# Chunked attention and a feed-forward layer on one core: weights in become float16 in the second group, those out in the third, on ACT and DVE

## The chip, the core and the metric

The kernel runs on one core of a Trainium2 chip. The core has five engines with instruction queues of their own: PE (TensorE, matmuls), DVE (VectorE), ACT (ScalarE), POOL (GpSimd) and SP (SyncE, which here issues all DMAs). The metric is device time in microseconds (us) of one execution; lower is better. One profiled execution of each kernel gives the rows that are read here. In them "PEld" is the loading of a matmul's stationary operand, a name such as `wh` is a tile with its buffer number left out, `out<-in` says what an instruction writes and reads, and L449 is line 449 of the kernel that the row is of.

## The reference

Attention inside chunks of 64 positions, followed by a feed-forward layer without bias over all 4608 tokens (8 batches of 576, with 8 heads of 64, so 512 features; 2048 hidden features), all in float32:

```python
scores = (q_c @ k_c.T) / sqrt(64)                 # per head and chunk of 64
attn = exp(scores - max(scores)); attn = attn / (sum(attn) + 1e-9)
x = (attn @ v_c)                                  # as [4608, 512]
h = x @ w_in                                      # [512, 2048]
g = h - tanh(h)
out = g @ w_out                                   # [2048, 512]
```

## The kernel before

The tokens are 36 tiles of 128, each a pair of chunks, in nine groups of four tiles (`SIZES`). In a group the hidden features are walked in 16 chunks of 128 (`fc`). For every chunk `gemm1` makes `ph` (128 hidden features by 512 tokens), `shrink` makes `t = h - tanh(h)` (tanh on ACT, subtraction on DVE) and splits it into a high part `gh` (ACT) and a low part `gl` (DVE), and `gemm2`, two chunks later (`LAG`), adds the chunk's product with `w_out` into four accumulators `po`, one for each tile. At the group's end `finish` copies the four accumulators out of PSUM (two on ACT, two on DVE) into tiles named `t` and stores them.

Single precision comes from two parts and three products: high by high, high by low, low by high. So a block of `gemm1` is 12 matmuls (3 products by 4 slices of the 512 features, L449) and a block of `gemm2` is 12 (3 products by 4 tiles, L478); both are 128x128 by 512. In groups 0 and 1 the parts are float32 tiles read as fp32r (`wt[fc][0]` and `[1]`, tiles `wh` and `wl`, each with both weights: part 0 of `w_in`, part 1 of `w_out`). From group 2 on all parts are float16, scaled by powers of two: the weights stand in `half_w[fc]`.

`Half.convert(fc)` makes those float16 weights, and all of them are made during group 1. For each of the two weights POOL adds the high and the low fp32r part back to one float32 (L405; into the attention's `s` buffers for the first three chunks, later into the `wl` tile of the chunk before, which is free by then), ACT rounds the scaled sum to the float16 high part (L409), and DVE takes the difference for the low part (L410), both into the `wh` tile. Two further freed `wl` tiles become second buffers of the attention's split `q` and `v`; POOL clears them (L259).

The attention of a group is computed during the group before it, in steps that stand between the blocks (`interleaved`): `sums` takes the spread of the next `q`, `k` (ACT, L99, whose elementwise result is thrown away into a tile named `a`) and `v` (DVE, L116), POOL takes the maximum over partitions (L106) and DVE makes scales of it (L110 to L112, L279); `split` makes float16 parts of `q` (L289, L290), `k` (L292, L293) and `v` (L298, L299); `scores` (L307, 24 matmuls); `softmax` (L313 to L321); `transpose` splits the weights into `a` (L327, L328) and has a DMA transpose it into an `s` tile (L330); `values` (L341, 24 matmuls) and L344, L345 write `x` for the next group. `k16` and `a` have one buffer each, `s` has two, `t` three.

The order of the first part is written out (`PLAN`); for the rest, and for ACT and DVE throughout, a scheduler places instructions by its own reckoning, and each engine then runs its list in order. PE's list before reads, at the start of each group, three blocks of L449 in a row, and from then on blocks of L478 and L449 by turns, with the attention's pieces between them. Before group 1 the weights are unpacked from 64-bit words (`weights`, L132 to L138): L137 (ACT) makes the high part and L138 (DVE) the low one, for one weight or for both at a time.

Of the kernel before, what the change touches and what calls it, by code (L numbers as in the profile page):

```python
# [22 lines left out]
P = 128  # L23
H = 8
# [32 lines left out]
def attn_ffn_kernel(ctx: ExitStack, tc: tile.TileContext, qE, kE, vE, qL, kL, vL, w_in, w_out, out):  # L57
# [19 lines left out]
    wt, half_w, w_pool = [[None, None] for _ in range(FC)], [None] * FC, {}  # L77

    def weight_tiles(pool, fcs):
        for fc in fcs:  # L80
            w_pool[fc] = pool
            for i, a in enumerate("hl"):
                wt[fc][i] = pool.tile([P, 2, DM], F32R, name=f"w{a}{fc}")
# [43 lines left out]
    def weights(pool, fc, parts):  # L127
# [8 lines left out]
        h, l = (t[:, parts] for t in wt[fc])  # L136
        nc.scalar.copy(out=h, in_=w.bitcast(F32))  # L137
        nc.vector.tensor_sub(l, w.bitcast(F32), h)  # L138
# [103 lines left out]
    class Late:  # L242
# [4 lines left out]
        def __init__(self, pool):  # L247
# [3 lines left out]
            self.v16, self.q16 = [], []  # L251
# [13 lines left out]
        def sums(self, g, n):  # L265
# [16 lines left out]
        def split(self, g, p, i):  # L282
# [8 lines left out]
            kk = d["k"] = self.pool.tile([P, 2, H, CH], F16, name="k16", bufs=1)  # L291
# [31 lines left out]
        def transpose(self, p):  # L323
# [5 lines left out]
            aT = self.pool.tile([P, H, CH], F32, name="s", bufs=2).bitcast(F16).rearrange("p h k -> p (h k)").rearrange("p (i q) -> p i q", i=8)  # L329
# [36 lines left out]
    class Half:  # L366
# [29 lines left out]
        def convert(self, fc):  # L396

            h, l = wt[fc]
            if fc < 3:
                w = [self.pool.tile([P, H, CH], F32, name="s", bufs=2).rearrange("p h k -> p (h k)") for _ in range(2)]  # L400
            else:
                t = w_pool[fc - 1].tile([P, 2, DM], F32R, name=f"wl{fc - 1}").bitcast(F32)
                w = [t[:, part] for part in range(2)]
            for part in range(2):
                nc.gpsimd.tensor_add(w[part], h[:, part].bitcast(F32), l[:, part].bitcast(F32))  # L405
            half = half_w[fc] = w_pool[fc].tile([P, 2, DM], F32R, name=f"wh{fc}").bitcast(F16).rearrange("p part (a n) -> p part a n", a=2)
            for part in range(2):
                to = self.to[:, part:part + 1]
                nc.scalar.activation(half[:, part, 0], w[part], AF.Copy, scale=to)  # L409
                nc.vector.scalar_tensor_tensor(out=half[:, part, 1], in0=w[part], scalar=to, in1=half[:, part, 0], op0=ALU.mult, op1=ALU.subtract)  # L410
# [16 lines left out]
    class FeedForward:  # L427
# [25 lines left out]
        def shrink(self):  # L453
            fc, t0, t1, n, ph = self.ph
            t = ffn.tile([P, MOST], F32, name="t", bufs=3)[:, :n]
            if self.half:
# [5 lines left out]
            if self.half:  # L462
# [50 lines left out]
    x, nx = new_x(), new_x()  # L513
    ff = FeedForward(0, x)
# [134 lines left out]
```

## Time and profile before

| | before |
| --- | --- |
| time, median of 3 runs | 886.29 us (885.56 to 889.21) |
| the profiled execution's own time | 889.29 us |
| its span, first to last instruction | 887.3 us |
| mean granted clock of PE | 0.989 |
| PE busy | 853.9 us (96%), 5163 matmuls |
| DVE busy | 597.3 us (67%) |
| ACT busy | 482.5 us (54%) |
| POOL busy | 60.4 us (7%) |
| DMA | 62.72 MB, mean 71 GB/s |

Busy times are shares of a program with unlike stages. Matmuls are pipelined, so a busy PE is not yet PE at its best pace; what a stage loses is seen in what PE waits for and in the granted clock, stage by stage. The columns of a group row ("engine op names shapes xcount | busy, mean ns | idle before, releaser") give in the last place how long the engine stood idle just before such instructions and what ended the idle time.

### The profile page before, as it was taken

Reading aid. Unit: us, or ns where it says so; the run is one execution under the profiler, and the core shown is the slowest. Engines: PE = TensorE matmul, PEld = TensorE weight load, DVE = VectorE, ACT = ScalarE, POOL = GpSimd, SP = SyncE. Lnnn points to the kernel's source line nnn. Section 1 sums busy time; section 2 is a strip of 40 time slices with the busy share of each in tenths; the row PEclk is TensorE's granted clock in tenths of the full one; section 3 lists DMA queues with packets and bytes.
Section 4 is the critical chain, followed back from the end, with each engine's and each line's share of the span. In section 5 each row is a group of like instructions: output and inputs, shape, how many; then the busy total and the mean of one; then the engine's idle time right before and its main releaser. Section 6 shows DMA issues by size and latency. Waiting matters only on the chain.

```text
span 887.3 us, 13178 instructions
## 1 busy us (share of the span) xinstructions
PE 853.9 (96%) x5163; PEld 487.2 (55%) x5165; DVE 597.3 (67%) x980; ACT 482.5 (54%) x840; POOL 60.4 (7%) x55
## 2 busy tenths in 40 slices
PE   9999999989689999999999999999999999999997
PEld 6888787867544544454445544454445444544443
DVE  6988795899978766667666766676666666543322
ACT  7798775654476537454645474447444744433222
POOL 0000011655310000000000000000000000000000
PEclk8999999999989999999999999999999999999999
DMA  9983434122123213111311132112221011001001
GB/s 236 256 211 110 160 120 142 48 50 59 24 74 82 60 36 107 37 49 36 106 48 49 36 84 70 49 37 60 84 60 37 13 49 24 13 13 48 1 1 48
DMA packets 61374, 62.72 MB, mean 71 GB/s; under 512 B 32640, under 2 KB 40832, under 8 KB 61312
## 3 DMA queue, kind: packets, MB, share of 16 engines
q1 hardware_dynamic: 61312, 61.88, 24.5%
q8 instruction: 40, 0.66, 0.3%
q14 instruction: 22, 0.18, 0.1%
HBM read 45.09 MB, written 9.44 MB: 61 GB/s over the span
## 4 chain that ended last, share of the span: by engine, by line
PE 68%; DVE 17%; DMA 5%; ACT 4%; issue 4%; SPq 1%; POOL 0%; ACTq 0%; POOLq 0%; DVEq 0%
PE ph L449 32%; PE po L478 30%; DVE wh L410 2%; DMA s<-a 2%; DMA out<-t 2%; PE psa L307 2%; PE psa L341 1%; PE psa L232 1%; ACT a L99 1%; DVE q16l L290 1%; DVE gl L470 1%; DVE v16l L299 1%; PE psa L184 1%; DVE t L461 1%; DMA k<-kE 1%
## 5 line engine op out<-in xcount | busy, mean ns | idle before, releaser
L449 PE MATMUL ph<-xh,wh 128*128 128x512 f16 (+2 forms) x1488 | 344.1, 379 | 9.3 <-DVE t L461 5.9
L478 PE MATMUL po<-wh,gh 128*128 128x512 f16 (+1 forms) x1024 | 319.2, 383 | 12.6 <-ACT gh L469 8.8
L478 PE MATMUL po<-wh,gl 128*128 128x512 f16 (+1 forms) x576 | 221.2, 385 | 2.9 <-DVE gl L465 2.9
L449 PEld LDWEIGHTS <-wh 128*128 128x128 f16 x1344 | 130.3, 98 | 157.9 <-issue 4.7
L457 ACT ACTIVATE t<-ph,sig 128x512 f32<-128x512 f32 x112 | 76.5, 683 | 139.1 <-PE ph L449 119.9
L458 DVE SCALAR_TENSOR_TENSOR t<-ph,sig,t 128x512 f32<-128x512 f32 x112 | 83.4, 745 | 96.6 <-ACT t L457 96.3
L478 PEld LDWEIGHTS <-gh 128*128 128x128 f16 x896 | 85.2, 98 | 103.1 <-ACT gh L464 6.3
L465 DVE SCALAR_TENSOR_TENSOR gl<-t,to_g,gh 128x512 f16<-128x512 f32 x112 | 84.1, 751 | 82.0 <-ACT gh L464 80.4
L464 ACT ACTIVATE gh<-t,to_g 128x512 f16<-128x512 f32 x112 | 80.7, 721 | 98.2 <-PE po L478 85.4
L478 PEld LDWEIGHTS <-gl 128*128 128x128 f16 x448 | 43.8, 98 | 57.6 <-DVE gl L465 5.4
L478 PE MATMUL po<-wl,gh 128*128 128x512 f32 x128 | 51.4, 402 | 0.0
L327 ACT CAST a<-s 128x512 f16<-128x512 f32 x28 | 17.3, 618 | 52.6 <-DVE s L321 52.6
L405 POOL TENSOR_TENSOR wl<-wh,wl 128x512 f32<-128x512 f32 x26 | 40.3, 1568 | 38.1 <-PE po L478 31.0
L449 PE MATMUL ph<-xh,wl 128*128 128x512 f32 (+1 forms) x144 | 36.3, 374 | 0.1
L449 PE MATMUL ph<-xl,wh 128*128 128x512 f32 (+1 forms) x144 | 36.2, 374 | 0.0
L469 ACT CAST gh<-t 128x512 fp32r<-128x512 f32 (+1 forms) x36 | 20.5, 570 | 24.6 <-DVE t L461 18.5
L106 POOL PARTITION_ALL_REDUCE xtop<-sums x7 | 2.6, 375 | 452.2 <-ACT a L99 446.1
L478 PEld LDWEIGHTS po<-wh,gh 128*128 128x128 f32 x128 | 24.6, 192 | 15.2 <-ACT gh L469 10.6
L449 PEld LDWEIGHTS ph<-xh,wh 128*128 128x128 f32 x144 | 24.8, 188 | 13.2 <-DVE t L461 7.2
L470 DVE TENSOR_TENSOR gl<-t,gh 128x512 fp32r<-128x512 f32 (+1 forms) x36 | 25.7, 713 | 7.1 <-ACT gh L469 6.8
L315 ACT ACTIVATE s<-s,exp 128x512 f32<-128x512 f32 x28 | 20.0, 713 | 18.5 <-DVE s L314 18.4
L449 PEld LDWEIGHTS ph<-xl,wh 128*128 128x128 f32 x144 | 26.0, 192 | 5.0
(120 smaller groups left out, 1068.1 us busy)
## 6 DMA issues: line engine op xcount, KB each, us to landing
out<-t SPq DMA_DIRECT2D x36, 256.0 KB, 2.2
raw<-w_in SPq DMA_DIRECT2D x16, 512.0 KB, 4.4
raw<-w_out SPq DMA_DIRECT2D x16, 512.0 KB, 6.8
rawk<-kL SPq DMA_DIRECT2D x28, 256.0 KB, 2.7
rawv<-vL SPq DMA_DIRECT2D x28, 256.0 KB, 2.6
xl<-qL SPq DMA_DIRECT2D x28, 256.0 KB, 2.7
qbd<-qE SPq DMA_DIRECT2D x16, 128.0 KB, 6.3
k<-kE SPq DMA_DIRECT2D x8, 256.0 KB, 6.0
```

The lines of the kernel that those rows point to most:

```text
L307: nc.tensor.matmul(ps[:, h], lhsT=q[a][:, h], rhs=d["k"][:, b, h], start=(k == 0), stop=(k == 2))
L315: nc.scalar.activation(s, s, AF.Exp, scale=d["exp"])
L405: nc.gpsimd.tensor_add(w[part], h[:, part].bitcast(F32), l[:, part].bitcast(F32))
L410: nc.vector.scalar_tensor_tensor(out=half[:, part, 1], in0=w[part], scalar=to, in1=half[:, part, 0], op0=ALU.mult, op1=ALU.subtract)
L449: nc.tensor.matmul(ph, lhsT=self.weight(fc, 0, a)[:, kc * P:(kc + 1) * P], rhs=x[b][:, kc, cols], start=(k == 0), stop=(k == 3 * KC - 1))
L457: nc.scalar.activation(t, ph, AF.Tanh, scale=self.sig)
L458: nc.vector.scalar_tensor_tensor(out=t, in0=ph, scalar=self.sig, in1=t, op0=ALU.mult, op1=ALU.subtract)
L464: nc.scalar.activation(gh, t, AF.Copy, scale=self.to_g)
L465: nc.vector.scalar_tensor_tensor(out=gl, in0=t, scalar=self.to_g, in1=gh, op0=ALU.mult, op1=ALU.subtract)
L469: nc.scalar.copy(out=gh, in_=t)
L470: nc.vector.tensor_sub(gl, t, gh)
L478: nc.tensor.matmul(self.po[t], lhsT=gg[a][:, ts], rhs=self.weight(fc, 1, b), start=(fc == 0 and i == 0), stop=(fc == FC - 1 and i == 2))
```

## The change

Weights are kept as one tile for each weight and part of a chunk (`wt[fc][part]` is a pair of tiles of 512 columns), where one tile held both weights. `weights` therefore makes high and low part of `w_in` and of `w_out` by instructions of their own.

`w_in` alone is converted in group 1, `w_out` in group 2. So group 2 runs its first product on float16 and its second on fp32r (`self.half` is a pair of flags). `convert` no longer has POOL add the parts: ACT makes the float16 high part from the scaled fp32r high part, DVE takes the difference, and a second DVE instruction adds the scaled fp32r low part to it. The result goes into the tile of the chunk before that held the low part (`place_of`), so the tiles of the high parts come free instead. Of the fourteen `w_in` tiles that are freed so, six become the attention's second buffers (`v16`, `q16`, and two for `k16`), two the places for its transposed weights (`aT`), four the places of the outputs (`outs`), one the place for L99's unused result (`junk`), and one the first place for `w_out`.

```diff
+            for part in range(2):
+                wt[fc][part] = [pool.tile([P, DM], F32R, name=f"w{a}{part}{fc}") for a in "hl"]
+    def place_of(a, part, fc, dtype=F16):
+        return w_pool[fc].tile([P, DM], F32R, name=f"w{a}{part}{fc}").bitcast(dtype)
...
-        h, l = (t[:, parts] for t in wt[fc])
-        nc.scalar.copy(out=h, in_=w.bitcast(F32))
-        nc.vector.tensor_sub(l, w.bitcast(F32), h)
+        for part in range(2)[parts]:
+            h, l = wt[fc][part]
+            w = ws[fc][:, part].bitcast(F32)
+            nc.scalar.copy(out=h, in_=w)
+            nc.vector.tensor_sub(l, w, h)
...
-                junk = self.pool.tile([P, 2, H * CH], F16, name="a", bufs=1).bitcast(U8).rearrange("p a (b n) -> p (a b) n", b=2)
+                junk = self.pool.tile([P, 2, H * CH], F16, name="a", bufs=1).bitcast(U8).rearrange("p a (b n) -> p (a b) n", b=2) if self.junk is None else self.junk
...
-            aT = self.pool.tile([P, H, CH], F32, name="s", bufs=2).bitcast(F16).rearrange("p h k -> p (h k)").rearrange("p (i q) -> p i q", i=8)
+            aT = self.aT[p % 2] if self.aT else self.pool.tile([P, H, CH], F32, name="s", bufs=2).bitcast(F16).rearrange("p h k -> p (h k)").rearrange("p (i q) -> p i q", i=8)
...
-                nc.gpsimd.tensor_add(w[part], h[:, part].bitcast(F32), l[:, part].bitcast(F32))
-            half = half_w[fc] = w_pool[fc].tile([P, 2, DM], F32R, name=f"wh{fc}").bitcast(F16).rearrange("p part (a n) -> p part a n", a=2)
-            for part in range(2):
-                to = self.to[:, part:part + 1]
-                nc.scalar.activation(half[:, part, 0], w[part], AF.Copy, scale=to)
-                nc.vector.scalar_tensor_tensor(out=half[:, part, 1], in0=w[part], scalar=to, in1=half[:, part, 0], op0=ALU.mult, op1=ALU.subtract)
+        def convert(self, part, fc, place):
+            half_w[part][fc] = place.rearrange("p (a n) -> p a n", a=2)
+            (h, l), (h16, l16), to = wt[fc][part], (half_w[part][fc][:, i] for i in range(2)), self.to[:, part:part + 1]
+            h, l = h.bitcast(F32), l.bitcast(F32)
+            nc.scalar.activation(h16, h, AF.Copy, scale=to)
+            nc.vector.scalar_tensor_tensor(out=l16, in0=h, scalar=to, in1=h16, op0=ALU.mult, op1=ALU.subtract)
+            nc.vector.scalar_tensor_tensor(out=l16, in0=l, scalar=to, in1=l16, op0=ALU.mult, op1=ALU.add)
...
+            self.half = g > 1, g > 2
...
-                ot = ffn.tile([P, DM], F32, name="t", bufs=3)
+                ot = outs[t] if outs else ffn.tile([P, DM], F32, name="t", bufs=3)
...
-                at[2 * fc + 2 * LAG + 1].append(lambda fc=fc: half.convert(fc))
-            at[2 * LAG + 4].append(lambda: att.room(half.spare(0), half.spare(1)))
+                at[2 * fc + 1].append(lambda fc=fc: half.convert(0, fc, place_of("l", 0, fc - 1) if fc else first_place))
...
+                t = [place_of("h", 0, fc) for fc in (range(6) if k == 0 else range(6, 13))]
+                if k == 0:
+                    att.room(t[0:2], t[2:4])
+                    att.k16 += [a.rearrange("p (a h c) -> p a h c", a=2, h=H) for a in t[4:6]]
+                else:
+                    att.aT += [a.rearrange("p (i q) -> p i q", i=8) for a in t[0:2]]
+                    outs.extend(a.bitcast(F32) for a in t[2:6])
+                    att.junk = t[6].bitcast(U8).rearrange("p (a n) -> p a n", a=MOST // P)
+            at[12].append(lambda: more(0))
+            at[2 * FC + 2].append(lambda: more(1))
+        if g == 2:
+            for fc in range(FC):
+                at[2 * fc + 2 * LAG + 1].append(lambda fc=fc: half.convert(1, fc, place_of("l", 1, fc - 1) if fc else place_of("h", 0, 13)))
```

Instructions move, because the scheduler decides anew. PE's list is the same from the start of group 1 on, block by block. Three other places follow; line numbers of the changed kernel are its own (L457 and L466 are the old L461 and L470, L408 and L409 the two new DVE conversions, L103 the old L99, L453 and L460 the old L457 and L464, L500 the old L504).

DVE in group 1, the first softmax of the attention there, before:

```order
L461 TENSOR_TENSOR t<-ph,t 128x512
L314 TENSOR_TENSOR s<-psa,mx 128x512
L293 SCALAR_TENSOR_TENSOR k_1802<-rawk,to,k_1802 128x512
L470 TENSOR_TENSOR gl<-t,gh 128x512
L317 TENSOR_REDUCE sm<-s 128x8
L410 SCALAR_TENSOR_TENSOR wh_1812<-wl_1809,to_w,wh_1812 128x512
L318 TENSOR_SCALAR sm<-sm 128x8
```

and now, to where the attention's `a` is made:

```order
L409 SCALAR_TENSOR_TENSOR wl_1851<-wl_95,to_w,wl_1851 128x512
L324 TENSOR_SCALAR sm<-sm 128x8
L296 SCALAR_TENSOR_TENSOR q16l<-xl,to,q16h 64x8x64
L466 TENSOR_TENSOR gl<-t,gh 128x512
L325 RECIPROCAL sm<-sm 128x8
L408 SCALAR_TENSOR_TENSOR wl_1890<-wh_98,to_w,wl_1890 128x512
L326 TENSOR_SCALAR sm<-sm 128x8
L299 SCALAR_TENSOR_TENSOR wh_1818<-rawk,to,wh_1818 128x512
L327 TENSOR_TENSOR s<-s,sm 128x512
L457 TENSOR_TENSOR t<-ph,t 128x512
L409 SCALAR_TENSOR_TENSOR wl_1890<-wl_99,to_w,wl_1890 128x512
L334 TENSOR_TENSOR a<-s,a 128x512
```

The conversions read the weights' own tiles instead of a sum from POOL, there are two for a chunk of one weight, and `a` (L334) stands behind the next chunk's subtraction and a conversion.

POOL in group 1, before:

```order
L405 TENSOR_TENSOR s<-wh_70,wl_71 128x512 x2
L106 ISA
L106 ISA xtop<-sums 128x3
L405 ISA
L405 TENSOR_TENSOR s<-wh_72,wl_73 128x512 x2
L259 MEMSET wl_1655 128x1024 x2
L259 MEMSET wl_1656 128x1024 x2
L405 TENSOR_TENSOR s<-wh_74,wl_75 128x512 x2
```

and now:

```order
L265 MEMSET wh_1814 128x1024
L265 MEMSET wh_1815 128x1024
L110 ISA xtop<-sums 128x3
L265 MEMSET wh_1816 128x1024
L265 MEMSET wh_1817 128x1024
```

The additions are gone, 32 in all; the maximum of the spreads (`xtop`) stands between MEMSETs.

ACT at the end of a group (3, with float16 on both products), before, from the spreads to the last `gh` (three rows of the attention and the copies of the outputs, L504, stand behind it):

```order
L99 ACTIVATE a,sums<-xl 128x2048
L99 ACTIVATE a,sums<-rawk 128x2048
L457 ACTIVATE t<-ph,sig 128x512
L289 ACTIVATE q16h<-xl,to 64x8x64 x2
L464 ACTIVATE gh<-t,to_g 128x512
L292 ACTIVATE k_4326<-rawk,to 128x512
L298 ACTIVATE v16h<-rawv,to 64x8x64
L457 ACTIVATE t<-ph,sig 128x512
L298 ACTIVATE v16h<-rawv,to 64x8x64
L289 ACTIVATE wl_1656<-xl,to 64x8x64 x2
L464 ACTIVATE gh<-t,to_g 128x512
```

and now the last two chunks:

```order
L453 ACTIVATE t<-ph,sig 128x512
L460 ACTIVATE gh<-t,to_g 128x512
L453 ACTIVATE t<-ph,sig 128x512
L460 ACTIVATE gh<-t,to_g 128x512
L304 ACTIVATE wh_1814<-rawv,to 64x8x64
L350 ACTIVATE xh<-psa 128x4x128
L304 ACTIVATE wh_1814<-rawv,to 64x8x64
L500 ACTIVATE wh_2453<-po_3418,undo_g 128x512
```

The spreads now stand in mid-group, at the eighth chunk or so, and the splits of the next group's pairs follow them there; the last two chunks have `t` and `gh` next to each other, and the outputs (`wh_2453`) have tiles of their own.

More of the change, by code (lines that the diff above doesn't have):

```diff
@@ L73, in attn_ffn_kernel @@
     ps_a = ctx.enter_context(tc.tile_pool(name="ps_a", bufs=2, space=PSUM))
-    wt, half_w, w_pool = [[None, None] for _ in range(FC)], [None] * FC, {}
+    wt, half_w, w_pool = [[None, None] for _ in range(FC)], [[None] * FC for _ in range(2)], {}
     def weight_tiles(pool, fcs):
@@ L427, in attn_ffn_kernel, with __init__ @@
     class FeedForward:
-        def __init__(self, g, x, half=None):
-            self.g, self.x, self.queue, self.po, self.half = g, x, [], [], half
-            if half:
+        def __init__(self, g, x):
+            self.g, self.x, self.queue, self.po = g, x, [], []
+            self.half = g > 1, g > 2
+            if g > 1:
                 self.sig, self.to_g, self.undo_g = half.power_of(g)
         def weight(self, fc, part, i):
-            return half_w[fc][:, part, i] if self.half else wt[fc][i][:, part]
+            return half_w[part][fc][:, i] if self.half[part] else wt[fc][part][i]
         def room(self, pool, tiles):
@@ L455, in shrink @@
             t = ffn.tile([P, MOST], F32, name="t", bufs=3)[:, :n]
-            if self.half:
+            if self.half[0]:
                 nc.scalar.activation(t, ph, AF.Tanh, scale=self.sig)
@@ L461, in shrink @@
                 nc.vector.tensor_sub(t, ph, t)
-            if self.half:
+            if self.half[1]:
                 gh, gl = (ffn.tile([P, MOST], F32R, name=f"g{a}").bitcast(F16)[:, :n] for a in "hl")
@@ L498, in finish @@
             for t in range(SIZES[self.g]):
-                ot = ffn.tile([P, DM], F32, name="t", bufs=3)
-                if self.half:
+                ot = outs[t] if outs else ffn.tile([P, DM], F32, name="t", bufs=3)
+                if self.half[1]:
                     if t % 2:
@@ L513, in attn_ffn_kernel @@
     x, nx = new_x(), new_x()
+    outs = []
     ff = FeedForward(0, x)
@@ L587, in attn_ffn_kernel @@
         for part in range(2):
-            nc.scalar.activation(junk, wt[fc][0][:, part].bitcast(F32), AF.Square, accum_out=sums_w[part][:, fc:fc + 1])
+            nc.scalar.activation(junk, wt[fc][part][0].bitcast(F32), AF.Square, accum_out=sums_w[part][:, fc:fc + 1])
     ff.finish()
@@ L595, in attn_ffn_kernel @@
         x, nx = nx, new_half_x() if g + 1 < NG else None
-        ff = FeedForward(g, x, half if g > 1 else None)
+        ff = FeedForward(g, x)
         ff.room(ps_o1, range(2))
```

19 lines of the change are left out of this document (4 added, 15 removed).

## The prediction

> **What bounds the kernel now.** I first cut the span into groups of four token tiles, since one busy share mixes stages with different limits. The cuts are the places where the trace has three L449 blocks in a row, which is how a group begins. Columns of the table by stretches: length, busy time with instruction count of PE, PEld, DVE, ACT and POOL, granted clock, DMA share, GB/s.
>
> ```profile
> core 0: us, PE busy (x) PEld busy (x) DVE busy (x) ACT busy (x) POOL busy (x), PEclk, DMA share, GB/s
> 141.25:256.64 115.39, 101.13 (x577) 79.30 (x575) 100.43 (x140) 66.23 (x105) 50.93 (x36) 0.96 0.20 52
> 160.68:239.90 79.22, 72.17 (x446) 56.94 (x444) 77.80 (x96) 44.44 (x72) 45.24 (x31) 0.98 0.21 50
> 256.64:347.82 91.18, 89.44 (x577) 43.17 (x577) 68.19 (x118) 54.74 (x81) 2.87 (x3) 1.00 0.25 70
> 347.82:438.95 91.13, 88.98 (x577) 43.02 (x576) 58.92 (x103) 47.71 (x71) 0.37 (x1) 1.00 0.20 59
> 438.95:529.61 90.66, 88.99 (x578) 43.01 (x576) 58.93 (x103) 47.72 (x71) 0.37 (x1) 1.00 0.21 59
> ...
> 710.93:799.41 88.48, 88.48 (x577) 43.16 (x576) 50.76 (x86) 38.14 (x58) 0.00 (x0) 1.00 0.10 25
> ```
>
> The rows are group 1, a piece of it, and groups 2, 3, 4 and 7 (5 and 6 repeat 4's 90.66). All have the same 577 matmuls. Group 7 runs PE without a pause: 88.48 us is the floor of a float16 group. Groups 2 to 6 are 2.2 to 2.7 us above it, group 1 is 26.9 us above. In group 1's inner 79 us DVE is busy 98% of the time: there DVE is the bound, elsewhere PE is.
>
> Next, what PE waits for, in group 1 (first three rows) and after it (last three): microseconds in total, times, longest.
>
> ```profile
> PE po L478 <- ACT gh L469: 7.2, 2, 4.2
> PE ph L449 <- DVE t L461: 5.9, 2, 3.1
> PE psa L341 <- DMA s<-a: 1.0, 1, 1.0
> ...
> PE po L478 <- ACT gh L464: 3.8, 5, 0.8
> PE po L478 <- DVE gl L465: 2.9, 5, 0.6
> PE ph L449 <- DVE t L458: 2.2, 5, 0.8
> ```
>
> Group 1 loses 14.1 us in five waits. It loses more than the waits: three stretches right behind the longest of them run at half clock (last of the columns but two), and PE's rows show one such idle time.
>
> ```profile
> 244.04 0.80 PE L478 MATMUL po<-wh,gh 128*128 128x512 f32 x1 [4.17 <-ACT gh L469]
> ...
> 185.85:189.26 3.41, 3.41 (x17) 2.42 (x16) 3.41 (x6) 1.14 (x3) 0.42 (x1) 0.50 0.26 77
> 243.88:247.29 3.41, 3.25 (x8) 2.47 (x9) 2.24 (x4) 1.34 (x3) 0.00 (x0) 0.50 0.40 77
> 254.12:257.53 3.41, 3.41 (x10) 1.97 (x9) 2.85 (x6) 2.07 (x5) 0.00 (x0) 0.50 0.27 104
> ```
>
> Three times 3.41 us at half speed cost 5.1 us. 115.39 - 14.1 - 5.1 = 96.2 us is what group 1 needs without them.
>
> **Why DVE is full.** The same DVE operations cost differently in group 1 (first two rows) and in group 4 (last two).
>
> ```profile
> L410 DVE SCALAR_TENSOR_TENSOR wh<-wl,to_w,wh 128x512 f16<-128x512 f32 x24 | 23.5, 1008 | 0.1
> L293 DVE SCALAR_TENSOR_TENSOR k<-rawk,to,k 128x512 f16<-128x512 f32 x4 | 4.0, 1010 | 0.0
> ...
> L465 DVE SCALAR_TENSOR_TENSOR gl<-t,to_g,gh 128x512 f16<-128x512 f32 x16 | 12.0, 751 | 9.5 <-ACT gh L464 9.2
> L293 DVE SCALAR_TENSOR_TENSOR k<-rawk,to,k 128x512 f16<-128x512 f32 x4 | 3.0, 739 | 0.0
> ```
>
> L293 is the same instruction at 739 and at 1010 ns. What differs is POOL, which adds halves of weights in group 1 (50.93 us busy) and rests later. The order of time shows that it is POOL's additions and not its clearing of buffers:
>
> ```profile
> 163.33 3.11 POOL L405 TENSOR_TENSOR s<-wh,wl 128x512 f32<-128x512 f32 x2 [7.05 <-DVE t L461]
> 166.38 3.62 POOL L259 MEMSET wl<- 128x1024 f16 x4
> ...
> 163.50 3.48 DVE L299 SCALAR_TENSOR_TENSOR v16l<-rawv,to,v16h 64x512 f16<-64x512 f32 x2
> 168.22 1.41 DVE L410 SCALAR_TENSOR_TENSOR wh<-s,to_w,wh 128x512 f16<-128x512 f32 x2
> ```
>
> Two operations beside two additions take 3.48 us; two beside the MEMSETs 1.41. The page "SBUF — State Buffer" of the Trainium skill (section "Who interferes with whom") says the same: a DVE operation with two SBUF inputs blocks only against a GpSimd operation that reads SBUF. The trace agrees (1.74 us each against 0.71).
>
> How much it is: group 4's DVE time, 58.93, plus 30 conversions at 0.751 (22.5) is 81.4 us. Measured are 100.43, so some 19 us in group 1 are lengthening.
>
> **The change, part by part.**
>
> (1) *Group 1.* All 32 POOL additions go. DVE keeps 32 conversion instructions there (two for each of 16 chunks instead of one for each of 32), so its work is 58.9 + 32 x 0.751 = 82.9 us against 96.2 us of PE: 86% where it was saturated. The new order spreads them two or three to a chunk, and a chunk's `gl` is wanted only four blocks of 12 matmuls (11 us) after its `ph`. POOL keeps four MEMSETs, which the row above clears of blame. I take all five waits and all half clocks as gone, but leave 0.8 us, for L341's wait hangs on a transposing DMA as much as on DVE: 97.0 us, which is -18.4. Bounds: 94.9 (32 blocks at 2.79 and eight attention pieces at 0.70, rows below; -20.5) and half of the loss staying (-9).
>
> (2) *Group 2.* The second product now runs on the unconverted fp32r weights. Chain of waits, a block of 12 in fp32r, one in float16, and an attention piece:
>
> ```profile
> 152.64 2.79 PE ph L449 x12
> ...
> 268.22 2.59 PE ph L449 x12
> 270.81 0.70 PE psa L307 x24
> ```
>
> 16 blocks x 0.20 = +3.2 us on PE, nothing hides that. The page "TensorE: Matmul & The Clock Gate" of the Trainium skill (section "Back-to-back issue gap") gives N/2.4 + 2.5 ns between matmuls without regard to the type, 216 ns for both; by it this term would be zero and the forecast 858 us. Here the rows say 216 (2.59/12) and 233 (2.79/12), and the rows decide.
>
> The 32 new DVE instructions (24.0 us) and 16 ACT ones go on top of group 4's load: 82.9 of DVE in some 92 us, 90%. PE covers them so long as DVE is not lengthened; with POOL idle it is not. If that cover failed, each microsecond of DVE over 92 would show. So group 2 is 88.48 + 3.2 + 0.5 for its edges = 92.2, or +1.0. Bounds: +0.3 and +13 (rival 2).
>
> (3) *Group edges.* The end of group 2 and the start of 3, on SP, ACT, DVE and PE:
>
> ```profile
> 329.09 1.23 SPq L330 DMA_TRANSPOSE s<-a  x1
> 332.22 1.91 ACT L99 ACTIVATE a<-xl 128x2048 uint8<-128x2048 f32 x1 [1.57 <-DMA s<-a]
> 336.81 0.17 DVE L110 TENSOR_SCALAR from<-xtop 128x3 f32<-128x3 f32 x1 [5.38 <-POOL xtop L106]
> 344.47 0.60 PE L478 MATMUL po<-wh,gh 128*128 128x512 f16 x2 [0.72 <-ACT gh L464]
> 345.65 0.39 PE L478 MATMUL po<-wh,gl 128*128 128x512 f16 x1 [0.58 <-DVE gl L465]
> 352.45 0.69 ACT L457 ACTIVATE t<-ph,sig 128x512 f32<-128x512 f32 x1 [4.39 <-DMA out<-t]
> 353.98 2.32 PE L449 MATMUL ph<-xh,wh 128*128 128x512 f16 x10 [0.81 <-DVE t L458]
> ```
>
> Two chains end here. L99 writes its unused result over `a` and so waits for the transposing DMA; behind it POOL's maximum and DVE's L110 are late (DVE stands 5.38 us), and the split of the next pair falls into the last two chunks, ahead of `gh`. And the outputs take the three `t` buffers, so the next group's first tanh waits 4.39 us for their DMAs. The change gives L99 a place of its own, and the ACT order shows it moved from two chunks before the end to mid-group, the splits with it; the outputs get four places. Late next: nothing up to group 7's floor. I take 89.0 us for groups 3 to 6, leaving 0.5 each: -2.1 for group 3, -1.7 for each of 4, 5 and 6. Bounds: 0 and 2.2 each.
>
> (4) *The end.* PE's last matmul and the last copy:
>
> ```profile
> 882.08 0.38 PE L478 MATMUL po<-wh,gl 128*128 128x512 f16 x1
> ...
> 883.46 0.75 DVE L502 TENSOR_SCALAR t<-po,undo_g 128x512 f32<-128x512 f32 x1 [1.50 <-DMA out<-t]
> ```
>
> PE is done at 882.46; the copy starts 1.0 later because its buffer waits for the first output's DMA. With four places: -1.0, nothing left to wait for but PE.
>
> (5) *The start.* Weight halves become separate tiles, so nine DVE subtractions of 1024 columns become 18 of 512:
>
> ```profile
> L138 DVE TENSOR_TENSOR wl<-w,wh 128x1024 fp32r<-128x1024 f32 x9 | 10.9, 1220 | 1.4 <-ACT wh L137 1.4
> L138 DVE TENSOR_TENSOR wl<-w,wh 128x512 fp32r<-128x512 f32 x14 | 9.5, 688 | 2.6 <-ACT wh L137 2.4
> ```
>
> 9 x (2 x 0.688 - 1.220) = 1.4 us more DVE work while it is nearly full, against an earlier start of the first product, which waits for one half only. Between -1 and +1.4 I take +0.5.
>
> Sum: 0.5 - 18.4 + 1.0 - 2.1 - 5.1 - 1.0 = -25.1. The profiled execution has a span of 887.3 and a time of 889.29, some 3 us over the median of 886.29; the difference is taken from the median: 861 us.
>
> **The rivals.**
>
> *Rival 1: only group 1 gains.* The edges stay, since the last `gh` and `gl` of a group are a chain of four dependent operations whatever stands before them. For it: PE's 0.72 + 0.58 there have no DMA in them. Against: group 7's edge has the same chain and no wait (88.48). Without the 7.2 us of part 3: 868 us.
>
> *Rival 2: DVE stays the bound.* The lengthening has another cause than POOL, perhaps the fp32r traffic, and follows the conversions into group 2. Then DVE needs 58.9 + 32 x 1.008 + 11.6 (what is left of the 19 us once the conversions' 30 x 0.257 are counted at their own) = 102.8 us in both groups, with two half-clock stretches (3.4) in each: group 1 106 (-9), group 2 106 (+15); with parts 3 to 5 (-7.7) 884 us, no change that can be told. Against it: the MEMSET row, and group 4's 739 ns.
>
> *Rival 3: slower, by late transposes.* In the new order the attention's `a` in groups 1 and 2 stands behind a conversion and the next chunk's subtraction, and its DMA takes 3 us more. If PE then stands at L341 for over 3 us, as in the 4.17 row, it also loses half of 3.41: 4.8 us a pair. It turns the sign when six of the eight pairs do so (6 x 4.8 = 29 > 25.1); with all eight 899 us. For it: the one L341 wait above. Against: that was 1.0 us with DVE saturated.
>
> *Rival 4: the change does not free POOL or the edges in time*, because the scheduler puts conversions where a place is not yet free. Each such wait would be a row of DVE waiting for PE; I see no such row in the new order, and give it a price of half of part 1: 870 us.
>
> **How the numbers follow.** Forecast 0.64; rival 1 0.16, rival 2 0.06, rival 3 0.05, rival 4 0.09. The predicted time is the forecast's, 861. Its own bounds reach from 855 (the floor in groups 1 and 3 to 6) to 866. The range takes in rivals 1 and 4 and some better luck at the start: 853 to 874. This kernel's runs can tell 0.5%, 4.4 us, from no change. Faster by more: forecast, rivals 1 and 4, and some of rival 2, 0.90. Within: the rest of rival 2 and little else, 0.05. Slower: rival 3, 0.05.
>
> **What would show it.** Right: POOL without additions; L293 near 740 ns in group 1; PE's waits in group 1 under 2 us in all and no stretch at clock 0.50 in it; group 1 near 97, group 2 near 92, groups 3 to 6 near 89; DVE's wait for `xtop` under 2 us; no tanh waiting for an output's DMA. Wrong: DVE operations still at 1 us in groups 1 or 2 (rival 2), the edges still at 90.7 (rival 1), waits of L341 for the transposing DMA (rival 3), DVE waiting for PE before a conversion (rival 4), or a group 1 that starts more than 2 us later than 141.25.

## The result, and the profile after

Measured side by side, before took 887.0 us (median of 4 runs, 885.56 to 889.21) and the changed kernel **860.42 us** (median of 4, 857.21 to 861.19): ratio 0.969, 95% interval 0.966 to 0.973. The forecast was 861. The profiled execution of the changed kernel took 861.19 us, with a span of 859.4 against 887.3 before.

The same cut into groups, at the three L445 blocks in a row (L445 is the old L449, L474 the old L478). The rows are groups 1, 2, 3, 4 and 7 and the rest; 5 and 6 are 88.48 too.

```profile
core 0: us, PE busy (x) PEld busy (x) DVE busy (x) ACT busy (x) POOL busy (x), PEclk, DMA share, GB/s
142.72:237.82 95.10, 95.10 (x577) 76.87 (x576) 88.02 (x162) 65.65 (x102) 5.20 (x6) 1.00 0.27 77
237.82:329.97 92.15, 92.15 (x578) 59.27 (x577) 77.14 (x133) 55.58 (x86) 0.37 (x1) 1.00 0.21 58
329.97:418.46 88.49, 88.49 (x578) 43.18 (x578) 59.32 (x100) 47.82 (x71) 0.37 (x1) 1.00 0.22 63
418.46:506.94 88.48, 88.48 (x578) 43.19 (x577) 59.34 (x101) 48.07 (x71) 0.37 (x1) 1.00 0.21 60
...
683.90:772.38 88.48, 88.48 (x578) 43.17 (x577) 49.32 (x82) 37.63 (x57) 0.00 (x0) 1.00 0.10 25
772.38:859.40 87.02, 83.04 (x385) 37.45 (x383) 26.29 (x35) 24.16 (x35) 0.00 (x0) 1.00 0.06 24
```

In groups 1 to 7 the length and PE's busy time are now one number, at clock 1.00: PE runs from 142.72 to its last matmul without a pause (the last row goes on for 4 us behind that matmul). These groups have the same matmuls and differ by the type that they multiply: both products in fp32r (95.10), the second alone (92.15), none (88.48). PE's list of waits holds 4.8 us in all (the two longest of its rows are shown; the other four are 2.5 of that):

```profile
PE ph L541 <- DVE warm L519: 1.2, 1, 1.2
PE po L474 <- ACT gh L465: 1.1, 3, 0.5
...
DVE from L114 <- POOL xtop L110: 3.2, 6, 0.6
```

These waits lie ahead of group 1, since from there to the last matmul PE is busy without a break. The last row is DVE's: L114 (the old L110) waited 0.6 us at most for POOL's maximum, where one such wait was 5.38 us. And the chain of work that ended last, on the profile's page, is PE's for 93% of the span, where it was 68% before:

```profile
PE 93%; DVE 5%; ACT 1%; issue 1%; DMA 0%; SPq 0%; DVEq 0%
```

DVE in group 1, by line, with the instructions that used to be lengthened:

```profile
L409 DVE SCALAR_TENSOR_TENSOR wl<-wl,to_w,wl 128x512 f16<-128x512 f32 x15 | 11.2, 747 | 0.1
L408 DVE SCALAR_TENSOR_TENSOR wl<-wh,to_w,wl 128x512 f16<-128x512 f32 x15 | 11.1, 739 | 1.0 <-ACT wl L407 1.0
L466 DVE TENSOR_TENSOR gl<-t,gh 128x512 fp32r<-128x512 f32 x16 | 10.9, 683 | 0.5 <-ACT gh L465 0.5
L457 DVE TENSOR_TENSOR t<-ph,t 128x512 f32<-128x512 f32 x16 | 10.9, 681 | 0.5 <-ACT t L456 0.4
L120 DVE TENSOR_REDUCE sums<-rawv 128x1 f32<-128x2048 f32 x2 | 4.6, 2286 | 1.4 <-DMA rawv<-vL 1.4
L296 DVE SCALAR_TENSOR_TENSOR q16l<-xl,to,q16h 64x512 f16<-64x512 f32 x6 | 4.5, 746 | 0.1
L296 DVE SCALAR_TENSOR_TENSOR wh<-xl,to,wh 64x512 f16<-64x512 f32 x6 | 4.5, 745 | 0.1
...
L299 DVE SCALAR_TENSOR_TENSOR wh<-rawk,to,wh 128x512 f16<-128x512 f32 x5 | 3.7, 746 | 0.1
```

L299 is the L293 of before: 746 ns here, 1010 there. Where the time went, from the two tables by groups (profiled executions):

| | before | after | difference | forecast |
| --- | --- | --- | --- | --- |
| start of group 1 | 141.25 | 142.72 | +1.5 | +0.5 |
| group 1 | 115.39 | 95.10 | -20.3 | -18.4 |
| group 2 | 91.18 | 92.15 | +1.0 | +1.0 |
| group 3 | 91.13 | 88.49 | -2.6 | -2.1 |
| groups 4 to 6, together | 271.98 | 265.44 | -6.5 | -5.1 |
| group 7 | 88.48 | 88.48 | 0 | 0 |
| group 8 to the end of the span | 87.9 | 87.02 | -0.9 | -1.0 |
| span | 887.3 | 859.4 | -27.9 | -25.1 |

### The profile page after: what moved, and what is told of

It reads as the page before. It is cut to its first block, busy times and chain, and to the rows that moved or that the text cites. A ratio compares the mean times of both kernels' runs of the same rounds, so it can differ in the third digit from the quotient of the medians.

```text
span 859.4 us, 13143 instructions
## 1 busy us (share of the span) xinstructions
PE 850.5 (99%) x5163; PEld 503.1 (59%) x5165; DVE 593.9 (69%) x1021; ACT 483.5 (56%) x849; POOL 12.2 (1%) x23
## 4 chain that ended last, share of the span: by engine, by line
PE 93%; DVE 5%; ACT 1%; issue 1%; DMA 0%; SPq 0%; DVEq 0%
PE po L474 42%; PE ph L445 41%; PE psa L347 2%; PE psa L313 2%; PE psa L190 2%; PE psa L238 1%; DVE w L138 1%; DVE w L139 1%; DVE wl L144 1%; PE ph L541 0%; DVE t L457 0%; DMA k<-kE 0%; PE psa L151 0%; ACT wh L143 0%; DVE gl L466 0%
## 5 line engine op out<-in xcount | busy, mean ns | idle before, releaser
L445 PE MATMUL ph<-xh,wl 128*128 128x512 f16 (+2 forms) x1404 | 323.9, 378 | 0.0
L474 PE MATMUL po<-wl,gh 128*128 128x512 f16 (+1 forms) x912 | 289.7, 382 | 0.0
L445 PEld LDWEIGHTS <-wl 128*128 128x128 f16 x1260 | 121.2, 98 | 144.8 <-issue 2.7
L454 DVE SCALAR_TENSOR_TENSOR t<-ph,sig,t 128x512 f32<-128x512 f32 x112 | 83.5, 746 | 107.2 <-ACT t L453 107.1
L453 ACT ACTIVATE t<-ph,sig 128x512 f32<-128x512 f32 x112 | 76.7, 685 | 140.1 <-PE ph L445 140.0
L474 PE MATMUL po<-wl,gl 128*128 128x512 f16 x360 | 136.4, 379 | 0.0
L461 DVE SCALAR_TENSOR_TENSOR gl<-t,to_g,gh 128x512 f16<-128x512 f32 x96 | 72.0, 750 | 80.7 <-ACT gh L460 80.0
L474 PEld LDWEIGHTS <-gh 128*128 128x128 f16 x768 | 73.4, 98 | 84.7
L460 ACT ACTIVATE gh<-t,to_g 128x512 f16<-128x512 f32 x96 | 69.1, 720 | 79.9 <-PE po L474 68.6
L474 PE MATMUL po<-wh,gh 128*128 128x512 f32 (+1 forms) x240 | 93.1, 404 | 1.1 <-ACT gh L465 1.1
L474 PE MATMUL po<-wh,gl 128*128 128x512 f32 (+1 forms) x216 | 84.2, 394 | 0.0
L474 PEld LDWEIGHTS <-gl 128*128 128x128 f16 x384 | 37.6, 98 | 45.3
L465 ACT CAST gh<-t 128x512 fp32r<-128x512 f32 (+1 forms) x52 | 30.4, 584 | 28.5 <-PE po L474 15.4
L474 PEld LDWEIGHTS po<-wh,gh 128*128 128x128 f32 x192 | 36.1, 188 | 10.1 <-ACT gh L465 2.2
L466 DVE TENSOR_TENSOR gl<-t,gh 128x512 fp32r<-128x512 f32 (+1 forms) x52 | 33.5, 645 | 11.3 <-ACT gh L465 9.2
L474 PEld LDWEIGHTS po<-wh,gl 128*128 128x128 f32 x192 | 35.9, 188 | 8.7 <-DVE gl L466 0.9
L474 PEld LDWEIGHTS po<-wl,gh 128*128 128x128 f32 x192 | 36.1, 188 | 7.2
L445 PE MATMUL ph<-xh,wh 128*128 128x512 f32 (+1 forms) x144 | 36.8, 376 | 1.0 <-ACT wh L143 1.0
L445 PE MATMUL ph<-xl,wh 128*128 128x512 f32 (+1 forms) x144 | 35.4, 367 | 0.0
L445 PEld LDWEIGHTS ph<-xh,wh 128*128 128x128 f32 x144 | 24.8, 188 | 6.8 <-ACT wh L143 2.5
```

The source lines that it names most:

```text
L445: nc.tensor.matmul(ph, lhsT=self.weight(fc, 0, a)[:, kc * P:(kc + 1) * P], rhs=x[b][:, kc, cols], start=(k == 0), stop=(k == 3 * KC - 1))
L453: nc.scalar.activation(t, ph, AF.Tanh, scale=self.sig)
L454: nc.vector.scalar_tensor_tensor(out=t, in0=ph, scalar=self.sig, in1=t, op0=ALU.mult, op1=ALU.subtract)
L460: nc.scalar.activation(gh, t, AF.Copy, scale=self.to_g)
L461: nc.vector.scalar_tensor_tensor(out=gl, in0=t, scalar=self.to_g, in1=gh, op0=ALU.mult, op1=ALU.subtract)
L465: nc.scalar.copy(out=gh, in_=t)
```

## The experiments

All are variants of the changed kernel, which was run again, on the chip of three of them (each cure of the edges undone alone, and the very last run): 860.48 us (median of 6, 857.5 to 861.07), groups 95.10, 92.15 and then 88.48 as before, so what follows is compared with 860.4 to 860.5 and with these group lengths. Its expectation was:

> The changed kernel itself, beside the others on the same chip. Both theories: 857 to 862 us, group 1 95.1 us, groups 3 to 7 88.5 us. Open: when group 1 starts. Before the change it started at 141.25 us; if the finer split of the weights costs time at the start (forecast: 0.5 us), the changed kernels start it later on the whole; if the start only varies from run to run, their starts lie on both sides of 141.25.

Its group 1 starts at 140.64 us, so the starts lie on both sides of 141.25 (step 5 below).

### POOL's additions put back, and POOL kept busy without reading

Theory: it is POOL's reading of SBUF that made DVE the bound of group 1. Rivals: the fp32r traffic, or POOL's work of any kind. The first run lets POOL add the parts again, and nobody reads the sum; the conversions stay the new ones.

```diff
+            def added(fc):
+                for part, a, b in ((0, 0, 384), (1, 0, 384), (0, 384, 512), (1, 384, 512)):
+                    h, l = (t[:, a:b].bitcast(F32) for t in wt[fc][part])
+                    nc.gpsimd.tensor_add(unread[:, :b - a], h, l)
...
+                at[2 * fc + 1].append(lambda fc=fc: added(fc))
```

> The changed kernel, with POOL adding again the high and low parts of every weight chunk in group 1, as many columns as before the change; nobody reads the sums. Theory (POOL's additions lengthen DVE's operations): the 128x512 float16 operations of DVE in group 1 go from about 740 ns to near 1000 ns on average, DVE's work in group 1 from some 84 us to about 100, more than PE's 95; PE waits in group 1 again, group 1 takes 100 to 112 us, the time is 866 to 878 us. Rival (the relief came from the new order and from spreading the conversions over two groups): DVE's operations stay at 740 ns, group 1 at 95 to 96 us, the time at 860 to 862 us.

The second has POOL clear the same tile instead, seven times for each chunk:

```diff
+            def cleared():
+                for _ in range(7):
+                    nc.gpsimd.memset(unread, 0.0)
...
+                at[2 * fc + 1].append(cleared)
```

> The changed kernel, with 112 MEMSETs of 384 float16 columns on POOL in group 1 into a tile that nobody reads, so that POOL is busy for about as long as with the additions, but reads nothing. Theory (it is POOL's reading that blocks DVE's operations with two inputs): DVE's operations stay near 740 ns, group 1 at 95 to 97 us, the time at 860 to 863 us. Rival (any work of POOL lengthens them): as with the additions, 866 to 878 us.

Measured: with additions **881.04 us** (880.86 to 882.47), with MEMSETs **860.56** (859.8 to 861.3). Group 1 by stretches, first with additions, then (second fence) with MEMSETs; columns as above.

```profile
140.97:257.49 116.52, 102.06 (x578) 81.25 (x576) 106.30 (x159) 63.99 (x99) 68.27 (x70) 0.94 0.21 58
```

```profile
141.40:236.50 95.10, 95.10 (x577) 76.88 (x576) 87.95 (x162) 65.87 (x102) 49.94 (x115) 1.00 0.27 77
```

POOL is busy for 68 and for 50 us, against 50.93 before the change. Clearing costs nothing, to the hundredth of a microsecond; the additions cost 21.4 us, all that group 1 had gained and a little more (64 smaller additions, of as many columns in all as the 32 of before, keep POOL busy for 68 us). DVE by line in that group, with the additions:

```profile
L466 DVE TENSOR_TENSOR gl<-t,gh 128x512 fp32r<-128x512 f32 x16 | 15.3, 957 | 2.3 <-ACT gh L465 2.2
L408 DVE SCALAR_TENSOR_TENSOR wl<-wh,to_w,wl 128x512 f16<-128x512 f32 x15 | 14.1, 941 | 1.5 <-ACT wl L407 1.5
L409 DVE SCALAR_TENSOR_TENSOR wl<-wl,to_w,wl 128x512 f16<-128x512 f32 x15 | 13.4, 890 | 0.1
L457 DVE TENSOR_TENSOR t<-ph,t 128x512 f32<-128x512 f32 x16 | 10.8, 681 | 3.3 <-ACT t L456 3.3
```

L408, L409 and L466 read two tiles of SBUF and went from 739, 747 and 683 ns to 941, 890 and 957. L457 stands between them, but one of its inputs is `ph` in PSUM: 681 ns, as without additions. The page "SBUF — State Buffer" of the Trainium skill (section "Who interferes with whom") states just this: a DVE operation with two SBUF inputs contends with a GpSimd operation that reads SBUF, not with one that only writes it, and a DVE operation with at most one SBUF input, outside the two-port modes, does not contend. The runs agree on all three (957 against 683 ns; 95.10 us with and without the MEMSETs; 681 ns for L457).

How 18 us more of DVE become 21 us of group 1 is in PE's waits of the run with additions:

```profile
PE psa L313 <- DVE wh L299: 5.6, 2, 3.3
PE ph L445 <- DVE t L457: 4.4, 1, 4.4
PE psa L313 <- ACT wh L298: 2.6, 1, 2.6
```

These 12.6 us, and half clock behind the long ones (granted clock 0.94 over the group; 6% of 116.5 is 7 us), make most of the 21.4. The theory stands, and both rivals fall: the fp32r traffic is in all these runs, and POOL's work without reading costs nothing. But the run with additions came out above the theory's own ranges (116.5 us against 100 to 112, 881 against 866 to 878), and not all of it is lengthening. An addition also holds the tiles that it reads, which a MEMSET does not: ACT's L298 stood 2.21 us until an addition was done, and PE's wait of 2.56 us for L298 ended right behind it; conversions (L407) stood 1.8 us for additions in three waits. That DVE's operations are lengthened is shown by their own rows; how much of the 21.4 us the lengthening makes alone is not.

### The group edges: the outputs' places, the spreads' place, the second buffers

The prediction had two chains there, each with its part of the 2.2 to 2.7 us: the late spreads (PE's waits for `gh` and `gl`) and the outputs in the `t` buffers (its wait for `t`). The rival: they are one chain. The changed kernel has both cures, so each is undone alone, and both together. First both, the outputs back in `t` and the spreads' result back in `a`:

```diff
-                    outs.extend(a.bitcast(F32) for a in t[2:6])
-                    att.junk = t[6].bitcast(U8).rearrange("p (a n) -> p a n", a=MOST // P)
```

> The changed kernel, with the outputs back in the three t buffers and the unused result of the spreads back in a; the rest stays. Theory (these two chains made the edges of the groups): the spreads move back behind the transposing DMA, groups 3 to 6 go from 88.5 to 90 to 91 us each, the end is 1 us later; the time is 867 to 871 us. Rival (the edges were freed by something else, the second buffers of k16 and of the transposed weights): groups 3 to 6 stay at 88.5 to 89 us, the time at 860 to 862 us.

Then the first line alone, and the second line alone:

> The changed kernel, with only the outputs back in the three t buffers (the spreads keep their own place). With both back, groups 3 to 6 took 91.4 us each. Theory (two independent chains): PE waits for t at each edge, 0.8 to 1.6 us, and not for gh and gl; groups 3 to 6 take 89.3 to 90.1 us, the end is 1 us later, the time is 864 to 868 us. Rival (one chain alone makes the edge, the other's wait is hidden in it): 91.4 or 88.5 us for groups 3 to 6.

> The changed kernel, with only the spreads' unused result back in a (the outputs keep their own places). Theory (two independent chains): the spreads stand two chunks before the group's end again, PE waits for the last gh and gl, 1.3 us at each edge, and not for t; groups 3 to 6 take 89.8 to 90.3 us, the time is 865 to 868 us. Rival (one chain alone makes the edge): 91.4 or 88.5 us for groups 3 to 6.

| | time, us | groups 3 to 6, us |
| --- | --- | --- |
| changed kernel | 860.48 (857.5 to 861.07) | 88.48 each |
| outputs back in `t` | 860.43 (860.38 to 862.22) | 88.48 each |
| spreads' result back in `a` | 869.9 (867.01 to 870.12) | 91.4, 90.2, 90.1, 90.2 |
| both back | 874.73 (873.37 to 876.25) | 91.4, 91.5, 91.2, 91.6 |

The outputs in three `t` buffers cost nothing at the edges by themselves. Only beside the late spreads do they cost something, 1.3 us in each of groups 4 to 6. PE's waits in the run with the spreads back, and (second fence) the row that differs with both back:

```profile
PE po L474 <- ACT gh L460: 2.9, 4, 0.8
PE po L474 <- DVE gl L461: 2.3, 4, 0.6
```

```profile
PE ph L445 <- DVE t L454: 6.1, 5, 1.6
```

The first two are the same with both back: 1.3 us at each of four edges. The wait for `t` (L454) is 1.0 to 1.3 us at the edges behind groups 3, 4 and 5 with both back, where it was about 0.3 before the change; so both back is 0.6 to 1.0 us a group slower there than before. Both undone, the groups came out above the theory (90 to 91 us; 874.73 us against 867 to 871). Alone, the spreads fit the theory of two chains in groups 4 to 6 (89.8 to 90.3), not its time (865 to 868), because groups 1 to 3 lengthened as well (95.81, 93.33 and 91.39 us). Alone, the outputs fit the rival (88.5). So there are two waits with one cause, and here are its rows at the end of group 3 and the start of 4, with both back (order of time: start, length, engine; idle time before and what ended it):

```profile
407.95 1.91 ACT L103 ACTIVATE a<-xl 128x2048 uint8<-128x2048 f32 x1 [1.54 <-DMA wh<-a]
412.55 0.17 DVE L114 TENSOR_SCALAR from<-xtop 128x3 f32<-128x3 f32 x1 [5.36 <-POOL xtop L110]
...
421.14 1.45 ACT L304 ACTIVATE wh<-rawv,to 64x512 f16<-64x512 f32 x2
422.62 1.26 ACT L500 ACTIVATE t<-po,undo_g 128x512 f32<-128x512 f32 x2
423.56 2.75 PE L445 MATMUL ph<-xh,first_place 128*128 128x512 f16 x12
424.51 4.49 SPq L506 DMA_DIRECT2D out<-t  x4
428.51 0.69 ACT L453 ACTIVATE t<-ph,sig 128x512 f32<-128x512 f32 x1 [4.63 <-DMA out<-t]
430.04 2.32 PE L445 MATMUL ph<-xh,wl 128*128 128x512 f16 x10 [1.13 <-DVE t L454]
```

The same place with only the outputs in `t`:

```profile
416.75 0.69 ACT L500 ACTIVATE t<-po,undo_g 128x512 f32<-128x512 f32 x1 [1.32 <-PE po L474]
417.46 3.83 SPq L506 DMA_DIRECT2D out<-t  x4
418.49 2.75 PE L445 MATMUL ph<-xh,first_place 128*128 128x512 f16 x12
421.28 0.69 ACT L453 ACTIVATE t<-ph,sig 128x512 f32<-128x512 f32 x1 [2.55 <-PE ph L445]
```

In the first fence L103 waits for the transposing DMA, the scales follow, and the splits, L304 the last of them, still occupy ACT when the outputs' copies are due. The first copy (L500) starts at 422.62, 0.9 us ahead of the next group's first block (423.56); its DMA goes out at 424.51, and the tanh stands 4.63 us for it. In the second fence the splits are long done: the copy starts 1.7 us ahead of the next group (416.75 against 418.49), as soon as PE is through with the accumulator, and the tanh waits for its matmuls alone. The late split makes both waits. So neither theory holds as it was stated: the spreads' wait stands by itself, the outputs' wait only behind it.

What is left of the attention's second buffers was undone in one run: one place for `k`'s float16 parts, and the transposed weights back in the two `s` buffers.

```diff
-            kk = d["k"] = self.k16[p % 2] if self.k16 else ...
+            kk = d["k"] = self.k16[p % len(self.k16)] if self.k16 else ...
...
-                    att.k16 += [a.rearrange("p (a h c) -> p a h c", a=2, h=H) for a in t[4:6]]
+                    att.k16 += [a.rearrange("p (a h c) -> p a h c", a=2, h=H) for a in t[4:5]]
...
-                    att.aT += [a.rearrange("p (i q) -> p i q", i=8) for a in t[0:2]]
```

> The changed kernel with one place for k's float16 parts from group 1 on (two in the change) and with the transposed weights back in the two s buffers that the softmax uses too, as before the change; v, q, the outputs' places and the spreads' own place stay. Theory (the edges are made by the spreads' late result alone, as the runs with the spreads' result back in a say, and the second buffers of k and of the transposed weights hide nothing that counts): groups 3 to 7 at 88.5 us, 860 to 862 us. Rival (these buffers carry part of the gain at the edges: with the transposed weights in s the softmax of the next pair must wait for the products of the pair before, and its own transposing DMA comes late): PE waits of 1 us or more at L347 (the product with v) for the DMA, or at L313 for DVE, one for each pair from group 2 on, 89.5 to 91 us a group, 866 to 874 us.

860.48 us (857.56 to 861.11), groups 3 to 7 at 88.5, no wait at L347 or L313: the theory holds. Three of the fourteen freed places are thus worth nothing in this order, four (the outputs') some 0.9 us at the very end (below), and one, L103's, carries the edges. The second buffers of `q` and `v`, which the kernel before had too, were not undone.

### Where w_out is converted

In the change, group 2 pays for fp32r weights. Theory of the first of two runs, which converts all of `w_out` in group 1 too: 64 conversions do not fit there. Only the places and the times differ:

```diff
-            self.half = g > 1, g > 2
+            self.half = g > 1, g > 1
...
-                t = [place_of("h", 0, fc) for fc in (range(6) if k == 0 else range(6, 13))]
+                t = [place_of("h", 0, fc) for fc in (range(6) if k == 0 else range(7, 14))]
...
-        if g == 2:
             for fc in range(FC):
-                at[2 * fc + 2 * LAG + 1].append(lambda fc=fc: half.convert(1, fc, place_of("l", 1, fc - 1) if fc else place_of("h", 0, 13)))
+                at[max(15 + fc, 2 * fc + 2 * LAG + 1)].append(lambda fc=fc: half.convert(1, fc, place_of("l", 1, fc - 1) if fc else place_of("h", 0, 6)))
```

> The changed kernel, with w_out converted in group 1 as well, in the new way and without POOL, so that group 2 runs on float16 for both products. Theory (DVE's capacity in group 1 sets the bound, and the spreading over two groups matters beside POOL's absence): DVE has 58.9 + 64 x 0.751 = 107 us of work in group 1 against 95 of PE; group 1 takes 105 to 112 us, group 2 falls from 92 to 88.5, the time is 867 to 875 us. Rival (POOL's absence alone is enough): group 1 takes 95 to 98 us, group 2 88.5, the time is 856 to 860 us, better than the change.

Measured: 860.7 us (858.61 to 866.23). Groups 1 and 2:

```profile
146.09:246.01 99.92, 97.79 (x578) 77.79 (x576) 94.40 (x165) 67.42 (x106) 4.66 (x5) 0.98 0.22 60
246.01:335.01 89.00, 88.65 (x578) 43.20 (x577) 71.36 (x128) 55.24 (x82) 1.25 (x2) 1.00 0.29 77
```

My theory missed: the two groups take 188.9 us, against 187.25 in the change; I had expected 105 to 112 for group 1 alone. The rival's 95 to 98, 88.5 and 856 to 860 us were missed too, by less. DVE is busy for 94.40 of 99.92 us and holds PE up in one long wait only: 1.96 us at 240.75, ended by ACT's `gh` (L465), which stood behind conversions that had waited for DVE. A stretch of 3.41 us at half clock begins right behind it and costs 1.7. The theory had added durations: 58.9 us of a group like 4 and 64 times 0.751 make 107. But recorded durations of DVE overlap. Four of its instructions in a row, from the run with both places back:

```profile
415.48 0.75 DVE L461 SCALAR_TENSOR_TENSOR gl<-t,to_g,gh 128x512 f16<-128x512 f32 x1
416.15 0.75 DVE L299 SCALAR_TENSOR_TENSOR wh<-rawk,to,wh 128x512 f16<-128x512 f32 x1
416.81 0.73 DVE L305 SCALAR_TENSOR_TENSOR v16l<-rawv,to,v16h 64x512 f16<-64x512 f32 x1
417.47 0.73 DVE L454 SCALAR_TENSOR_TENSOR t<-ph,sig,t 128x512 f32<-128x512 f32 x1
```

They start 0.66 to 0.67 us apart and are recorded with 0.73 to 0.75. In a full DVE an instruction of this kind took 0.66 us. This run says something on the change itself: of the 19.3 us that groups 1 and 2 gain by it (206.6 to 187.25), 17.7 come with all of `w_out` converted in group 1 too. That `w_out` waits for group 2 brings little (1.7 us between the profiles, and a median that does not tell the two apart).

The second run puts half of `w_out` into group 1, and the other half into the first half of group 2, ahead of its use; group 2 is then all float16:

```diff
-            self.half = g > 1, g > 2
+            self.half = g > 1, g > 1
...
+            for fc in range(FC // 2):
+                at[15 + fc].append(lambda fc=fc: half.convert(1, fc, place_of("l", 1, fc - 1) if fc else place_of("h", 0, 6)))
...
+            for fc in range(FC // 2, FC):
+                at[2 * (fc - FC // 2) + 1].append(lambda fc=fc: half.convert(1, fc, place_of("l", 1, fc - 1)))
```

> The changed kernel, with the conversion of w_out's first eight chunks in group 1 and of its last eight in the first half of group 2, ahead of their use there, so that group 2 runs on float16 for both products. With all 16 chunks in group 1 that group took 99.9 us (2.0 of it one wait, 1.7 a stretch at half clock) and group 2 89.0. Theory (POOL's absence frees DVE enough for 48 conversions in group 1): group 1 takes 95.1 to 96 us, group 2 88.5 to 89, 3 us less than the change in both; the time is 856 to 858.5 us. Rival (DVE's order in group 1 fails already with 48): group 1 at 97 us or more, no gain, 860 us or more.

```profile
142.93:239.37 96.44, 95.28 (x577) 76.78 (x576) 92.32 (x165) 65.25 (x102) 5.28 (x6) 1.00 0.23 63
239.37:327.86 88.49, 88.49 (x577) 43.17 (x577) 73.11 (x128) 57.37 (x86) 0.37 (x1) 1.00 0.27 76
```

```profile
PE psa L347 <- DMA s<-a: 1.2, 1, 1.2
```

The first fence has groups 1 and 2, the second a row of what PE waited for. **857.43 us** (856.9 to 859.07; ratio to before 0.966, interval 0.963 to 0.968). Group 2 is at the floor, and group 1 pays 1.3 us, of which the wait at L347 for the transposing DMA is 1.2. The time and group 2 are the theory's; group 1 lies between its 96 and the rival's 97. Together 184.9 against 187.25 us, 2.3 less; the medians, of runs on the same chip, differ by 3.05. It is the fastest of all kernels run here, by little: the slowest of its times, 859.07, is above the lowest of the changed kernel's, 857.21.

## Why the prediction was right, step by step

**What bounds.** As forecast, DVE bound group 1 and PE the rest; without POOL's additions PE bounds everything from group 1 on.

**(1) Group 1, -18.4 forecast, -20.3 measured.** The lengthening is shown from both sides, by taking the additions away and by putting them back. The 0.8 us that I left for L341's wait (now L347) were not lost; 95.10 lies 0.2 above my lower bound, which was the sum of PE's blocks. The other 1.1 us are in the 96.2, which was too high. Its 5.1 us for half clock was itself too large by 0.4, since the third stretch ends at 257.53 and group 1 at 256.64; so some 1.5 us of what group 1 lost stood in no term, and what they were is open. The working was less good than its sum: DVE's 82.9 us came out at 88.02, with 162 instructions where group 4 has 101 and the conversions add 32. Some half of the 29 others are attention work of the neighbouring pairs, which the new order pulls into group 1 (two spreads of `v`, L120, instead of one; twelve low parts of `q`, L296, instead of eight); the others are scales and two conversions of `w_out`. There was room for it: 93% busy, and no wait.

**(2) Group 2, +1.0 forecast and measured, by two errors that cancel.** The fp32r term was 3.2 and is 92.15 - 88.48 = 3.67; the 0.5 for edges did not come. Blocks from the chain of waits of the changed kernel, in group 2:

```profile
254.76 2.60 PE ph L445 x12
257.37 2.80 PE po L474 x12
...
268.18 0.70 PE psa L313 x24
268.88 2.90 PE po L474 x12
```

L445 is float16 there and L474 fp32r: 0.20 more, as I had taken it from group 1; but 0.3 in three blocks that stand behind an attention piece, of which I had counted none. That is 0.3 of the 0.47 us that were missing; the rest is in no single row.

**(3) The edges, -7.2 forecast, -9.2 measured.** The direction and the first chain were right. The step that failed is "Two chains end here": the outputs' wait was no cause of its own (88.48 us with the outputs back in `t`), but what the late split did to ACT. That its 0.8 us would go was right, and the place of its own for L103 would have been enough. The 0.5 us a group kept back were not needed; the groups went to group 7's floor, as the step itself said ("nothing up to group 7's floor").

**(4) The end, -1.0 forecast, -0.9 measured.** The last copy no longer waits for a DMA. In the changed kernel, and (second fence) with the outputs back in `t`:

```profile
855.04 0.38 PE L474 MATMUL po<-wl,gl 128*128 128x512 f16 x1
855.46 0.75 DVE L498 TENSOR_SCALAR wh<-po,undo_g 128x512 f32<-128x512 f32 x1 [0.55 <-PE po L474]
```

```profile
855.07 0.38 PE L474 MATMUL po<-wl,gl 128*128 128x512 f16 x1
856.43 0.75 DVE L498 TENSOR_SCALAR t<-po,undo_g 128x512 f32<-128x512 f32 x1 [1.49 <-DMA out<-t]
```

The outputs' places bring the copy 0.9 us nearer (0.42 behind the start of the last matmul instead of 1.36). A median cannot show it (860.43 against 860.48).

**(5) The start, +0.5 forecast, +1.5 measured, and not to be told.** Over the ten profiles of kernels with the changed start, group 1 begins between 140.64 and 146.09 us; before, in its one profile, at 141.25. The spread between executions is larger than the term. The +1.5 also compares unlike executions: before's profile had a stretch of 6.8 us at half clock from 8.4 us on. Four of the ten had such a stretch and begin group 1 at 140.64 to 141.84, around 141.25; five had none and begin at 142.40 to 142.93, the changed kernel's first profile among them; the one at 146.09 had 13.7 us of it. Like against like, no cost of the finer split is seen. Why the executions with the short stretch are the earlier ones is open.

**The rivals.** Rival 1 (edges stay) is excluded by 88.48. Rival 2 (lengthening of another cause) by the two POOL runs (its 11.6 us should read 11.3 by its own numbers, which moves its price by under 1 us). Rival 3 (late transposes) did not happen in the change; its first sign, a wait of 1.2 us at L347, came where group 1 was filled further. Rival 4 (conversions that wait for a place) cost nothing: its sign, DVE waiting for PE before a conversion, has no row (L408 waited 1.0 us in all for ACT, L409 0.1); ACT's half of the conversion, L407, waited 1.1 us in all for PE, and PE for none of it.

**The sum.** -25.1 forecast, -27.9 by the profiles, -26.6 by the medians: the parts kept back for what might remain (0.8, 0.5 a group) were too cautious.

## What to carry to other kernels

When an engine is full in one stage, compare the same instruction's mean time there and in a quiet stage before counting its instructions: here 18 us of group 1's DVE time came back with POOL's additions, and two conversions on DVE alone cost the group less than one whose sum came from POOL. Waits of unlike engines at one edge can have one cause; undo the cures one at a time and together before each gets its own term. Count a full engine by the distance between starts, not by recorded durations.

## What the runs showed of the hardware that was not expected

- DVE instructions with one input in PSUM kept their 681 ns beside POOL's additions, while those with both in SBUF went from 683 to 957 ns; MEMSETs that kept POOL busy for as long as before the change cost group 1 nothing.
- A 128x128 by 512 matmul with its weight load took 216 ns from start to start in float16 and 233 in fp32r (blocks of 12 in 2.59 and 2.79 us): 192 of them made 3.67 us of group 2, 19 ns each. The prediction weighed this against the page "TensorE: Matmul & The Clock Gate" of the Trainium skill (section "Back-to-back issue gap"), whose N/2.4 + 2.5 ns, there the gap of an isolated matmul, has no place for the type; the measured group says that the rows were right.
- DVE's recorded durations (0.75 us) overlap by some 0.08 us when its instructions follow each other without a wait.
- The part ahead of group 1, with the same instructions, varied by 5.5 us between executions, and not by the granted clock alone (142.72 us at a clock of 1.00, 140.64 at 0.98).
- Half clock can follow a shorter idle time of PE than the 3 us that the prediction's rival 3 asked for: with all of `w_out` converted in group 1, an idle time of 1.96 us was followed by 3.41 us at a granted clock of 0.50, while one of 2.78 us before the change was not.
